# Other places for the hidden weights, a second head with its decay rows in place, and two paced loads

## The chip, the cores and the metric

The kernel runs on one NeuronCore of a Trainium2 chip. The metric is the device time of one execution in microseconds (us). An execution's time is a little longer than the span of its profile, which goes from the first to the last instruction that the profile shows. PE is the matmul engine (TensorE), PEld its weight loads, DVE VectorE, ACT ScalarE, POOL GpSimd, and SP the engine that here issues every DMA.

## The reference

Three layers follow one another, on 4 batches of 576 positions with 512 channels:

```
attention, 8 heads of 64 (32 heads in all):
    cum    = cumsum(max(s, 0))
    scores = q k^T / 8 + min(-(cum_i - cum_j), 0), causal
    x      = softmax(scores) v
gate:      y = (sigmoid(causal conv of x, 5 taps) * (x w_val)) w_out
mixing:    u = y + (y^T U V)^T          over positions, rank 32
MLP:       out = u + relu(u w_ch1) w_ch2        512 -> 2048 -> 512
```

The float64 weights come as pairs of 32-bit words; the kernel widens them itself. For accuracy, most operands are split into a high part (fp32r) and a low part (the rest), and a product takes three matmuls: high by high, high by low, low by high.

## The kernel before

**Attention, heads one after the other.** In step n of one loop the scores of head n and the transposes of head n - 1 are issued, with the products with V after every second head. The decay is folded into the score matmul: each head's Q1 and K1 tiles hold 64 rows of q or k and, from partition 64 on, rows made from cum (K = 68 in all, 4 of them decay rows; 66 for head 0, 2 of them). `score` (L474) makes for each of five row blocks a score matmul into one of six PSUM buffers, a DVE instruction that masks and takes the maximum (a custom DVE operation in the profile, with its result `nm`), and an exponential on ACT; `trans` transposes the result on PE and copies it out. Small fill matmuls go with the transposes up to head 8.

**The decay rows.** For head 0 the row of s is loaded into two partitions (`first`, L239), clipped, scanned, and written into Q1 and K1 in place by two DVE instructions (`row`, L309). For the rest, all 32 rows are clipped, scanned and split on the DVE (L260 to L264), with two multiplications on ACT (L263, L265), in tiles E and F. Heads 1 and 2 get their rows by a DMA straight from E and F (L297, `direct`), the later ones from a copy in DRAM (`ef`).

**The first eight heads** (and two more) take q and k as they are, in `WHOLE`. For the others, `load_raw` (L276) loads q and k into one tile `qk`, ACT rounds it to `hi`, POOL subtracts, and five DMAs (`put`) move the parts into Q1, K1, Q2 and K2. The calls for heads 8 and 9 stand in steps 6 and 7; nothing in the program holds them back before that.

**The order of the work** on each engine isn't the program's. A planner plays the program through with estimated times: each engine takes, of what is ready, what has the highest priority. Priorities follow the program, raised or lowered by kind of work by `PLAN` and, in the first steps, `FIRST`. `later` holds work that the program itself defers. So work without a dependence can move far ahead, and on the chip each engine then keeps the planned order.

**Dense stage and MLP.** For each batch `values`, `outputs` and the mixing run beside the attention of the next, that of the last batch beside the first six MLP blocks. The MLP has 16 hidden blocks m of 128 in groups of 2, 2, 3, 4, 3, 2; within a group it goes through 5 token blocks t (four of 512, one of 256). `ch1` takes u of block t, split into uh and ul by POOL (`split_u`), with w1 of block m; `ch2`, two steps later, multiplies by w2 into accumulators. `widen_w` (L833) makes the four tiles w1h, w1l, w2h, w2l of block m, in ring place m mod 7. Each passes ACT (scale), POOL (limit), DVE (four steps), POOL (round to the high part), POOL (subtract), POOL (low part); it uses two scratch tiles of `scr0` and one of `scr1`, shared by all pieces in program order.

**Memory.** `w0` holds ring places 0 and 1 and is there from the beginning. `wb` (right side) is opened when the values of the last batch are done, and takes the place of their tiles. `ml` (left side) is opened when the dense stage of the last batch is issued, and takes the place of its tiles, in this order: the identity (0.5 KB a partition), w_out high and low (8 KB each), U4 (2.5 KB), V4 high and low (2.3 KB each), the gated values, nh and nl. A tile in `wb` or `ml` waits only for the tiles that stood at its own bytes. Tiles get their place in the order of allocation; `ml` begins with the eight tiles of u for t = 3 (2 KB each).

Of the kernel before, what the change touches and what calls it, by code (L numbers as in the profile page):

```python
# [11 lines left out]
F32 = mybir.dt.float32  # L12
F32R = mybir.dt.float32r
BF16 = mybir.dt.bfloat16
U32 = mybir.dt.uint32
AF = mybir.ActivationFunctionType
ALU = mybir.AluOpType
# [3 lines left out]


PLAN = {
    "pace": ("gpsimd", -500),
    "qk_hi": ("scalar", 6000),
    "qk_lo": ("gpsimd", 2000),
    "put": ("sync", 3000),
# [54 lines left out]
RING = 7  # L82
# [7 lines left out]
ORDER = "T0 T1 S0 T2 T3 S1 S2 S3 T4 S4 A0 A1"  # L90
NPD = 6
DT = {"exp": 0.51, "xh": 0.96, "xl": 0.25, "tap": 1.5, "taps": 0.9, "tanh": 1.83, "gv": 4.3, "nl": 3.6, "rows": 10.0, "prep": 1.51}
WARM = 13


@with_exitstack
def fused_kernel(ctx, tc, qT, kT, vP, s, wval, wout, convw, U, V, w1, w2, rows01, out):
    nc = tc.nc
    B, H, D, S = qT.shape
    P = 128  # L100
# [7 lines left out]
    KP = 4  # L108
# [5 lines left out]
    NH = B * H  # L114
# [99 lines left out]
    w0 = ctx.enter_context(tc.tile_pool(name="w0", bufs=1, side="right", reuse_waits="tile"))  # L214
    at = ctx.enter_context(tc.tile_pool(name="at", bufs=2, side="right"))
# [15 lines left out]
    def part(b, m, n=S, parts=P):  # L231
        return uT[0:parts, m, b * S:b * S + n]

    sp, cum = (part(1, m, parts=NH) for m in range(2))
    ones, first = part(1, 2), part(1, 3)
    E = [part(2, r, parts=NH) for r in range(KP)]
    F = [part(3, r, parts=NH) for r in range(KP)]
    coef = at1.tile([P, 4], F32, name="coef")
    nc.sync.dma_start(first[64:66, :], s[0, 0:1, :].to_broadcast([2, S]))  # L239
    nc.sync.dma_start(coef[64:66, :], rows01)  # L240
    nc.sync.dma_start(sp, s.rearrange("b h s -> (b h) s"))

# [10 lines left out]
    )  # L253
    nc.vector.memset(ones, 1.0)

    nc.vector.tensor_scalar_max(first[64:66, :], first[64:66, :], 0.0)
    nc.vector.tensor_tensor_scan(first[64:66, :], ones[64:66, :], first[64:66, :], 0.0, op0=ALU.mult, op1=ALU.add)
    for t, v in ((E[0], 8.0), (E[2], 8.0), (F[1], 1.0), (F[3], 1.0)):
        nc.gpsimd.memset(t, v)
    nc.vector.tensor_scalar_max(sp, sp, 0.0)  # L260
    nc.vector.tensor_tensor_scan(cum, ones[0:NH, :], sp, 0.0, op0=ALU.mult, op1=ALU.add)
    nc.vector.tensor_copy(F[0].bitcast(F32R), cum)
    nc.scalar.mul(E[1], F[0], -8.0)  # L263
    nc.vector.tensor_sub(F[2].bitcast(F32R), cum, F[0])  # L264
    nc.scalar.mul(E[3], F[2], -8.0)  # L265
    EF = [uT[0:NH, :, b * S:(b + 1) * S] for b in (2, 3)]


# [3 lines left out]
    hd = {}  # L272

    raw = {}

    def load_raw(n):  # L276

        if n < NH and n not in WHOLE:
            b, h = divmod(n, H)
            raw[n] = at.tile([P, S], F32, tag="qk", name="qk")  # L280
            nc.sync.dma_start(raw[n][0:64, :], qT[b, h])
            nc.sync.dma_start(raw[n][64:, :], kT[b, h])

    def load_head(n, direct=False):
        b, h = divmod(n, H)
        t = hd[n] = {"K": 64 + KP if n else 66, "nm": at.tile([P, 6], F32, tag="nm", name="nm")}
        kind = F32 if n in WHOLE else F32R
        for nm in ("Q1", "K1"):
            t[nm] = at.tile([64 + KP, S], kind, tag=nm, name=nm)
        if n in WHOLE:  # L290
            nc.sync.dma_start(t["Q1"][0:64, :], qT[b, h])
            nc.sync.dma_start(t["K1"][0:64, :], kT[b, h])
        else:
            t["qk"] = raw.pop(n)
        if n:
            for i, nm in enumerate(("Q1", "K1")):
                nc.sync.dma_start(t[nm][64:, :].bitcast(F32), EF[i][n:n + 1] if direct else ef[n, i])  # L297

# [5 lines left out]
    def prep_head(n):  # L304

        t = hd[n]
        if n == 0:
            def row(o, i):
                nc.vector.tensor_scalar(  # L309
                    o[64:66, :], first[64:66, :], coef[64:66, 2 * i:2 * i + 1], coef[64:66, 2 * i + 1:2 * i + 2],  # L310
                    op0=ALU.mult, op1=ALU.add,
                )
            return [lambda: row(t["Q1"], 0), lambda: row(t["K1"], 1)]
        if n in WHOLE:
            return []
        t["Q2"], t["K2"] = (at.tile([P, S], F32R, tag=nm, name=nm) for nm in ("Q2", "K2"))
        hi, lo = at.tile([P, S], F32R, tag="hi", name="hi"), t["Q2"]

        def put(o, i):
            Via("put").dma_start(o.bitcast(F32), i.bitcast(F32))  # L320

        def high():
            put(t["Q1"][0:64, :], hi[0:64, :])
            put(t["K1"][0:64, :], hi[64:, :])
            put(t["K2"][0:64, :], hi[64:, :])

        def low():

            put(t["K2"][64:, :], lo[64:, :])
            put(t["Q2"][64:, :], hi[0:64, :])  # L330
        return [
            lambda: rnd("qk_hi", hi, t["qk"]),
            lambda: rest("qk_lo", lo, t["qk"], hi),
            high,
            low,
        ]

    load_head(0)
    load_head(1, True)
    for i in range(2):  # L340
        nc.sync.dma_start(ef[:, i], EF[i])

    for f in prep_head(0):
        f()
    for c in range(5):
        for x in Pt[c]:
            nc.gpsimd.memset(x[:, 0 if c == 0 else CW[c]:], 0.0)
# [33 lines left out]
    def words(ap):  # L381

        return ap.bitcast(U32)
# [40 lines left out]
    pace = []  # L424
# [20 lines left out]
    w12 = {m: {x: w0.tile([P, 512], F32R, tag=f"{x}{m}", name=x) for x in ("w1h", "w1l", "w2h", "w2l")} for m in range(2)}  # L445
# [306 lines left out]
    for n in range(NH + 1):  # L752
        phase[0] = n
        if n > 0:
            pace[:] = [hd[n - 1]["nm"][:, 4:5]]
        if 2 <= n + 1 < NH:
            load_head(n + 1, n == 1)
        load_raw(n + 2)
        if n == 1:
            nc.sync.dma_start(craw.bitcast(U32), words(convw))  # L760
        if 1 <= n <= 3:
            load_wide(n - 1)
        if n < NH and n % 2:
            load_values(n)
        m = n - 1
        items = []

        def add(cost, f, *a):
            items.append((cost, f, a))

        ahead, before = n < NH, n > 0
        for x in (ORDER if m % 2 else ORDER0).split():
            kind, i = x[0], int(x[1])
            if kind == "S" and ahead:
                add((0.1, 0.22, 0.32, 0.42, 0.53)[i], score, n, i)
            elif kind == "T" and before:
                add((0.03, 0.21, 0.32, 0.43, 0.55)[i], trans, m, i)
            elif kind == "A" and before and m % 2:
                add((0.96, 1.7)[i], attn_v, m, i)
        if before and m % 2 == 1:  # L780
            add(0.0, norm, m // 2)
        total = sum(x[0] for x in items)
        if before and m % 2 == 1:
            defer(DT["rows"], lambda pr=m // 2: norm_rows(pr))
        if n + 1 < NH:
            for i, f in enumerate(prep_head(n + 1)):
                defer(DT["prep"] * i, f, "prep")
        todo = 0.0
        if dense:
            first, _, done, _ = dense[0]  # L790
            slots = max(1, first + H - n)
            todo = max(0.0, (DENSE - done) / slots)
        clock["dense"] = clock["att"] = 0.0
        for cost, f, a in items:
            f(*a)
            advance(cost)
            clock["att"] += cost
            if n > 0:
                steps[0] += SIDE[(n > 8) + (n > 12) + (n > 17)] * cost / total
                side_step(int(steps[0]))  # L800
                steps[0] -= int(steps[0])
            run_dense(todo * clock["att"] / total)
        if before and m % H == H - 1:
            dense.append([n + 1, dense_work(m // H), 0.0, clock["now"] + DWAIT])
        force("prep")
        if m % 2:
            hd.pop(m, None)
            hd.pop(m - 1, None)
# [11 lines left out]
    TW = 512  # L820
# [10 lines left out]
            nc.sync.dma_start(raws[k].bitcast(U32), words(w2)[m * P:(m + 1) * P, :] if k % 2 else words(w1)[m])  # L831

    def widen_w(m):  # L833
        pool = w0 if m % RING < 2 else wb if m % RING < 4 else ml
        d = w12[m] = {x: pool.tile([P, TW], F32R, tag=f"{x}{m % RING}", name=x) for x in ("w1h", "w1l", "w2h", "w2l")}

        def part(nm, k):
            scr = [wa.tile([P, TW], F32, tag=f"scr{k}", name=f"scr{k}", bufs=2 - k) for k in range(2)]
            steps = widen(pairs(raws.pop(k)), scr, hi=d[nm + "h"], lo=d[nm + "l"])

            return steps[:6] + [lambda: load_w(k + 2)] + steps[6:]
        return [
            lambda: part("w1", 2 * m), lambda: part("w2", 2 * m + 1),
            lambda: ready.add(m),
        ]
# [97 lines left out]
    wb = ctx.enter_context(tc.tile_pool(name="wb", side="right", **reuse))  # L943
# [6 lines left out]
    ml = ctx.enter_context(tc.tile_pool(name="ml", side="left", **reuse))  # L950
# [50 lines left out]
```

## Time and profile before

| | |
|---|---|
| three timed runs | 766.26, 769.34 (median), 770.9 us |
| the profiled execution | 764.93 us |
| its span | 762.8 us |
| mean granted clock of PE | 0.993 of full speed |
| PE busy | 743.7 us (98%) |
| DVE, ACT, POOL busy | 464.4, 299.2, 291.2 us |

The timed runs and the profiled execution are different executions of the same program. A busy time counts from the start of an instruction to its end; matmuls overlap, so a busy PE is not a PE at its peak. In the views below a line of the timeline has start, duration, engine, line, operation, output <- inputs, shape and count; a bracket at its end is the idle time of the engine just before it and what ended it. L132 is the line of a helper that issues most operations, so they are told apart by their tiles.

### The profile page before, as it was taken

Reading aid. Unit: us, or ns where it says so; the run is one execution under the profiler, and the core shown is the slowest. Engines: PE = TensorE matmul, PEld = TensorE weight load, DVE = VectorE, ACT = ScalarE, POOL = GpSimd, SP = SyncE. Lnnn points to the kernel's source line nnn. Section 1 sums busy time; section 2 is a strip of 40 time slices with the busy share of each in tenths; the row PEclk is TensorE's granted clock in tenths of the full one; section 3 lists DMA queues with packets and bytes.
Section 4 is the critical chain, followed back from the end, with each engine's and each line's share of the span. In section 5 each row is a group of like instructions: output and inputs, shape, how many; then the busy total and the mean of one; then the engine's idle time right before and its main releaser. Section 6 shows DMA issues by size and latency. Waiting matters only on the chain.

```text
span 762.8 us, 12349 instructions
## 1 busy us (share of the span) xinstructions
PE 743.7 (98%) x4453; PEld 624.8 (82%) x4453; DVE 464.4 (61%) x1052; ACT 299.2 (39%) x785; POOL 291.2 (38%) x321
## 2 busy tenths in 40 slices
PE   8999999899999999999899999999999999999998
PEld 4777888788887998798788888888888888888887
DVE  6798875887657755666749996424582234223234
ACT  4777756875677776633212211111121011001110
POOL 3466754553522233557197765102540024100000
PEclk9999999999999999999999999999999999999999
DMA  5734544644455432021103221100120000000023
GB/s 147 229 120 120 140 118 114 174 119 127 120 124 134 122 100 56 18 85 55 56 1 111 83 87 53 54 1 28 55 85 1 0 28 1 1 0 1 1 111 138
DMA packets 27012, 59.40 MB, mean 78 GB/s; under 512 B 4654, under 2 KB 5294, under 8 KB 26952
## 3 DMA queue, kind: packets, MB, share of 16 engines
q1 hardware_dynamic: 26952, 58.62, 26.9%
q8 instruction: 35, 0.57, 0.3%
q14 instruction: 25, 0.20, 0.1%
HBM read 37.04 MB, written 5.31 MB: 56 GB/s over the span
## 4 chain that ended last, share of the span: by engine, by line
PE 85%; DMA 4%; DVE 4%; ACT 3%; issue 2%; SPq 1%; POOL 0%; ACTq 0%; DVEq 0%
PE d L132 39%; PE acc L132 26%; PE pt L132 8%; PE av L132 6%; PE sc L132 6%; DMA qk<-in_kT 2%; DMA K<-Q 1%; DVE av L604 1%; ACT P L132 1%; DVE P L132 1%; DMA Q<-hi 1%; DVE uT L132 1%; DMA uT<-in_w 0%; ACT PTB L132 0%; ACT hi L132 0%
## 5 line engine op out<-in xcount | busy, mean ns | idle before, releaser
L132 PE MATMUL d<-u,w1h 128*128 128x512 f32 (+1 forms) x640 | 184.2, 371 | 0.0
L132 DVE SCALAR_TENSOR_TENSOR hl<-d,hh 128x512 fp32r<-128x512 f32 (+1 forms) x80 | 50.7, 635 | 170.3 <-ACT hh L861 170.3
L861 ACT ACTIVATE hh<-d 128x512 fp32r<-128x512 f32 (+1 forms) x80 | 44.2, 554 | 274.6 <-PE acc L132 149.5
L132 PEld LDWEIGHTS d<-u,w1h 128*128 128x128 f32 x640 | 116.0, 188 | 22.2
L132 PE MATMUL d<-u,w1l 128*128 128x512 f32 (+1 forms) x320 | 118.6, 371 | 0.0
L132 PE MATMUL acc<-hl,w2h 128*128 128x512 f32 (+1 forms) x320 | 105.0, 371 | 0.0
L132 PE MATMUL acc<-hh,w2h 128*128 128x512 f32 (+1 forms) x320 | 104.4, 372 | 0.5 <-DVE uT L132 0.5
L132 PE MATMUL acc<-hh,w2l 128*128 128x512 f32 (+1 forms) x320 | 102.0, 371 | 0.0
L132 ACT ACTIVATE P<-P,nm 64x64 f32<-64x64 f32 (+4 forms) x160 | 89.0, 560 | 25.2 <-DVE nm L132 24.6
L132 PE MATMUL sc<-K,Q 68*128 68x288 f32 (+11 forms) x384 | 89.1, 344 | 4.6 <-ACT PTB L132 1.8
L132 DVE CUSTOM_DVE_ANT_0 P<-sc,causal 64x64 f32<-64x64 f32 (+4 forms) x160 | 65.2, 421 | 30.8 <-PE sc L132 28.2
L132 PE MATMUL pt<-ident,P 128*128 128x128 f32 x480 | 78.5, 284 | 5.4 <-ACT PTA L139 2.6
L132 DVE TENSOR_TENSOR uT<-acc,uT 128x512 f32<-128x512 f32 (+1 forms) x120 | 70.1, 630 | 22.3 <-PE acc L132 22.2
L132 PEld LDWEIGHTS sc<-K,Q 68*128 68x128 f32 (+2 forms) x384 | 62.2, 193 | 13.2 <-ACT PTB L132 2.6
L132 PEld LDWEIGHTS d<-u,w1l 128*128 128x128 f32 x320 | 60.2, 188 | 11.0
L132 PEld LDWEIGHTS acc<-hh,w2h 128*128 128x128 f32 x320 | 58.7, 188 | 12.1 <-issue 0.9
L132 PEld LDWEIGHTS acc<-hl,w2h 128*128 128x128 f32 x320 | 58.8, 188 | 11.2
L132 PEld LDWEIGHTS acc<-hh,w2l 128*128 128x128 f32 x320 | 58.6, 188 | 11.3
L132 PEld LDWEIGHTS pt<-ident,P 128*128 128x128 f32 x480 | 56.3, 145 | 12.3 <-ACT PTA L139 3.6
L604 DVE SCALAR_TENSOR_TENSOR av<-X,cw,av 128x576 f32<-128x576 f32 x64 | 52.3, 817 | 4.9 <-ACT av L132 4.5
L132 DVE SCALAR_TENSOR_TENSOR scr<-raw,scr 128x512 uint32<-128x512 uint32 (+1 forms) x56 | 52.4, 936 | 1.4
L132 DVE TENSOR_SCALAR scr<-scr 128x512 uint32<-128x512 uint32 x56 | 43.3, 773 | 11.9 <-POOL w1l L132 6.3
(123 smaller groups left out, 1286.9 us busy)
## 6 DMA issues: line engine op xcount, KB each, us to landing
raw<-in_w SPq DMA_DIRECT2D x28, 512.0 KB
K<-hi SPq DMA_DIRECT2D x44, 144.0 KB
Q<-hi SPq DMA_DIRECT2D x44, 144.0 KB
V<-in_vP SPq DMA_DIRECT2D x16, 320.0 KB
out<-uT SPq DMA_DIRECT2D x16, 256.0 KB
qk<-in_qT SPq DMA_DIRECT2D x22, 144.0 KB
qk<-in_kT SPq DMA_DIRECT2D x22, 144.0 KB
K<-Q SPq DMA_DIRECT2D x22, 144.0 KB
```

Source lines behind the costliest of these rows:

```text
L132: return f(*args, **kw)
L604: Via("tap").scalar_tensor_tensor(g, X[:, k:k + S], cw[:, p, k:k + 1], g, op0=ALU.mult, op1=ALU.add,)
L861: Via("hh").activation(h_, o, AF.Relu)
```

## The change

- The four tiles of a hidden block stand together no more: in ring places 2 to 6, w2h and w2l are in `wb`, w1h and w1l in `ml`. Before, places 2 and 3 were in `wb` and places 4 to 6 in `ml`, all four tiles of each.
- Head 1 gets its two decay rows in place, as head 0 does, with its own row of s, loaded with head 0's at the start (K = 66). The clipping of these rows and of the 32 rows moves from DVE to ACT. The rows of both heads are issued ahead of the chain for the 32 rows.
- The raw loads of heads 8 and 9 are issued in steps 3 and 4, and each stands behind a POOL copy of one column that reads the last maximum of head 2 or 3.
- 10 instead of 13 warm-up matmuls, and priority 0 for the copies of kind "pace".

```diff
-    "pace": ("gpsimd", -500),
+    "pace": ("gpsimd", 0),
...
-WARM = 13
+WARM = 10
...
-    ones, first = part(1, 2), part(1, 3)
+    ones = part(1, 2)
+    first = [part(0, 0), part(0, 1)]
...
-    nc.sync.dma_start(first[64:66, :], s[0, 0:1, :].to_broadcast([2, S]))
+    for i in range(2):
+        nc.sync.dma_start(first[i][64:66, :], s[0, i:i + 1, :].to_broadcast([2, S]))
...
-    nc.vector.tensor_scalar_max(first[64:66, :], first[64:66, :], 0.0)
-    nc.vector.tensor_tensor_scan(first[64:66, :], ones[64:66, :], first[64:66, :], 0.0, op0=ALU.mult, op1=ALU.add)
-    for t, v in ((E[0], 8.0), (E[2], 8.0), (F[1], 1.0), (F[3], 1.0)):
-        nc.gpsimd.memset(t, v)
-    nc.vector.tensor_scalar_max(sp, sp, 0.0)
-    nc.vector.tensor_tensor_scan(cum, ones[0:NH, :], sp, 0.0, op0=ALU.mult, op1=ALU.add)
-    nc.vector.tensor_copy(F[0].bitcast(F32R), cum)
-    nc.scalar.mul(E[1], F[0], -8.0)
-    nc.vector.tensor_sub(F[2].bitcast(F32R), cum, F[0])
-    nc.scalar.mul(E[3], F[2], -8.0)
+    for x in first:
+        nc.scalar.activation(x[64:66, :], x[64:66, :], AF.Relu)
...
             raw[n] = at.tile([P, S], F32, tag="qk", name="qk")
+            if H <= n < H + 2:
+                Via("pace").tensor_copy(raw[n][:, 0:1], hd[n - H + 2]["nm"][:, 4:5])
...
-        if n:
+        if n > 1:
             for i, nm in enumerate(("Q1", "K1")):
...
-        if n == 0:
+        if n < 2:
+            x = first[n][64:66, :]
...
-            return [lambda: row(t["Q1"], 0), lambda: row(t["K1"], 1)]
+            return [
+                lambda: nc.vector.tensor_tensor_scan(x, ones[64:66, :], x, 0.0, op0=ALU.mult, op1=ALU.add),
+                lambda: row(t["Q1"], 0), lambda: row(t["K1"], 1),
+            ]
...
-    load_head(0)
-    load_head(1, True)
+    for n in range(2):
+        load_head(n)
+    for n in range(2):
+        for f in prep_head(n):
+            f()
+    for t, v in ((E[0], 8.0), (E[2], 8.0), (F[1], 1.0), (F[3], 1.0)):
+        nc.gpsimd.memset(t, v)
+    nc.scalar.activation(sp, sp, AF.Relu)
+    nc.vector.tensor_tensor_scan(cum, ones[0:NH, :], sp, 0.0, op0=ALU.mult, op1=ALU.add)
+    nc.vector.tensor_copy(F[0].bitcast(F32R), cum)
+    nc.scalar.mul(E[1], F[0], -8.0)
+    nc.vector.tensor_sub(F[2].bitcast(F32R), cum, F[0])
+    nc.scalar.mul(E[3], F[2], -8.0)
     for i in range(2):
         nc.sync.dma_start(ef[:, i], EF[i])
-
-    for f in prep_head(0):
-        f()
...
-        load_raw(n + 2)
+        if 3 <= n <= 4:
+            load_raw(n + H - 3)
+        elif n + 2 >= H + 2:
+            load_raw(n + 2)
...
-        if n + 1 < NH:
+        if 2 <= n + 1 < NH:
             for i, f in enumerate(prep_head(n + 1)):
...
-        pool = w0 if m % RING < 2 else wb if m % RING < 4 else ml
-        d = w12[m] = {x: pool.tile([P, TW], F32R, tag=f"{x}{m % RING}", name=x) for x in ("w1h", "w1l", "w2h", "w2l")}
+        d = w12[m] = {
+            x: (w0 if m % RING < 2 else wb if x[1] == "2" else ml).tile([P, TW], F32R, tag=f"{x}{m % RING}", name=x)
+            for x in ("w1h", "w1l", "w2h", "w2l")
+        }
```

## Rows read from the trace of the kernel before

**Rows 1.** The page: busy time by engine, and the chain that ended last.
```profile
PE 743.7 (98%) x4453; PEld 624.8 (82%) x4453; DVE 464.4 (61%) x1052; ACT 299.2 (39%) x785; POOL 291.2 (38%) x321
...
PE 85%; DMA 4%; DVE 4%; ACT 3%; issue 2%; SPq 1%; POOL 0%; ACTq 0%; DVEq 0%
```

**Rows 2.** Stretches: PE, PEld, DVE, ACT, POOL busy (count), PE's granted clock, DMA share, GB/s.
```profile
12.50:16.00 3.50, 3.50 (x16) 2.96 (x17) 0.59 (x4) 1.96 (x9) 0.00 (x0) 0.51 0.98 231
107.00:116.00 9.00, 7.38 (x43) 6.76 (x41) 5.67 (x17) 6.44 (x18) 3.42 (x4) 0.81 0.37 83
...
380.00:402.00 22.00, 22.00 (x114) 18.50 (x113) 10.54 (x21) 2.90 (x6) 19.07 (x23) 1.00 0.04 13
```

**Rows 3.** Timeline of the first 12 us: head 0's rows, scores, maximum, first transpose.
```profile
3.67 1.35 DVE L257 TENSOR_TENSOR_SCAN uT<-uT 2x576 f32<-2x576 f32 x1
...
6.28 0.57 DVE L309 TENSOR_SCALAR K<-uT,coef 2x576 f32<-2x576 f32 x1
...
6.90 3.08 PE L132 MATMUL sc<-K,Q 66*128 66x64 f32 x12 [0.34 <-DVE K L309]
...
8.73 0.68 ACT L263 ACTIVATE uT<-uT 32x576 f32<-32x576 f32 x1 [6.72 <-DVE uT L262]
8.73 0.75 DVE L264 TENSOR_TENSOR uT<-uT 32x576 fp32r<-32x576 f32 x1
...
9.41 0.20 DVE L132 CUSTOM_DVE_ANT_0 P<-sc,causal 64x64 f32<-64x64 f32 x1
...
10.11 0.67 ACT L132 ACTIVATE hi<-qk 128x576 fp32r<-128x576 f32 x1
...
11.16 0.33 PE L132 MATMUL pt<-ident,P 128*128 128x128 f32 x1 [0.96 <-ACT P L132]
```

**Rows 4.** The chain of waits in the first 25 us: start, duration, what held it.
```profile
0.74 1.45 DMA uT<-in_s
...
12.81 4.17 DMA K<-Q
```

**Rows 5.** Timeline: head 1's first score, the next rounding, a transpose behind it.
```profile
12.47 0.60 PE L132 MATMUL sc<-K,Q 68*128 68x64 f32 x2 [0.98 <-DVE nm L132]
...
21.08 0.68 ACT L132 ACTIVATE hi<-qk 128x576 fp32r<-128x576 f32 x1 [1.72 <-DMA qk<-in_kT]
...
22.47 0.66 PE L132 MATMUL pt<-ident,P 128*128 128x128 f32 x4 [0.69 <-ACT P L132]
```

**Rows 6.** Timeline of PE: a gap later in the attention.
```profile
109.79 0.81 PE L132 MATMUL sc<-K,Q 68*128 68x288 f32 x4 [1.61 <-ACT PTB L132]
```

**Rows 7.** PE: last reads of U4 and V4h; matmuls with w1h before 401.2 us.
```profile
377.77 0.39 PE L132 MATMUL d<-nl,U 128*128 128x512 f32 x1
...
381.58 0.29 PE L132 MATMUL d<-V4h,ast 128*128 128x288 f32 x1
...
L132 PE MATMUL d<-u,w1h x80: 277/393/401, 337.9 to 401.0; 128*128 128x512 f32 x64, 128*128 128x256 f32 x16
```

**Rows 8.** Timeline of POOL: weights of hidden blocks 2 to 4, splits of u.
```profile
339.47 0.62 POOL L132 TENSOR_SCALAR w1h<-scr 128x512 fp32r<-128x512 f32 x1
...
362.11 1.71 POOL L132 TENSOR_TENSOR scr<-scr,w2h 128x512 f32<-128x512 f32 x1
...
381.11 2.09 POOL L132 TENSOR_SCALAR u<-uT 128x512 fp32r<-128x512 f32 x4 [13.75 <-DVE uT L703]
383.17 0.62 POOL L132 TENSOR_SCALAR w1h<-scr 128x512 fp32r<-128x512 f32 x1
...
390.15 1.29 POOL L132 TENSOR_TENSOR scr<-scr,w1h 128x512 f32<-128x512 f32 x1
391.40 3.94 POOL L132 TENSOR_TENSOR u<-uT,u 128x512 fp32r<-128x512 f32 x4
```

**Rows 9.** Timeline of the DVE: one step of the widening, twice.
```profile
361.20 0.47 DVE L132 TENSOR_SCALAR scr<-scr 128x512 uint32<-128x512 uint32 x1
...
362.60 1.50 DVE L132 TENSOR_SCALAR scr<-scr 128x512 uint32<-128x512 uint32 x1
```

More of the change, by code (lines that the diff above doesn't have):

```diff
@@ L285, in load_head @@
         b, h = divmod(n, H)
-        t = hd[n] = {"K": 64 + KP if n else 66, "nm": at.tile([P, 6], F32, tag="nm", name="nm")}
+        t = hd[n] = {"K": 64 + KP if n > 1 else 66, "nm": at.tile([P, 6], F32, tag="nm", name="nm")}
         kind = F32 if n in WHOLE else F32R
@@ L306, in prep_head @@
         t = hd[n]
-        if n == 0:
+        if n < 2:
+            x = first[n][64:66, :]
             def row(o, i):
                 nc.vector.tensor_scalar(
-                    o[64:66, :], first[64:66, :], coef[64:66, 2 * i:2 * i + 1], coef[64:66, 2 * i + 1:2 * i + 2],
+                    o[64:66, :], x, coef[64:66, 2 * i:2 * i + 1], coef[64:66, 2 * i + 1:2 * i + 2],
                     op0=ALU.mult, op1=ALU.add,
                 )
-            return [lambda: row(t["Q1"], 0), lambda: row(t["K1"], 1)]
+            return [
+                lambda: nc.vector.tensor_tensor_scan(x, ones[64:66, :], x, 0.0, op0=ALU.mult, op1=ALU.add),
+                lambda: row(t["Q1"], 0), lambda: row(t["K1"], 1),
+            ]
         if n in WHOLE:
```

## The prediction

> **What bounds it.** I read the page first: TensorE's matmul queue (PE) is busy for 98% of the span [rows 1], so any change can only win idle PE time or time at the lower clock. I then cut the span into stretches, to see where the 19 us that are left lie and where the granted clock drops. At 12.5 to 16 us PE is always busy but at a granted clock of 0.51, that is, mostly at 1.2 GHz instead of 2.4; the same drop stands in the stretch from 107 to 116. From 380 to 402 us PE is busy throughout while POOL is busy 19.07 of 22 us [rows 2]. The timeline of the first 11 us shows why the start is slow: the first scores start at 6.90, when the DVE has written head 0's second row, and the first maximum (the custom DVE instruction) starts only at 9.41, when the DVE is through with the chain for all 32 rows [rows 3]. The chain of waits then runs through the loads and moves of head 8, whose turn comes after seven others: 4.17 us of a K<-Q move at 12.81 [rows 4]. So the start is bound by latency, the rest by PE, and the change touches the start and one transition, 380 to 402.
>
> **Head 0.** Before, the DVE clips the row (relu), scans it and writes two rows; now ScalarE clips. The row of s lands at 0.74 + 1.45 = 2.19 [rows 4]. A relu of two rows on ACT is not in the trace; nearest is ACT's pass over 32 rows of the same length, 0.68 [rows 3], so 2.9. Scan 1.35 and two rows of 0.57 each [rows 3] give 5.4 instead of 6.85. One more small load now stands ahead of head 0's Q and K on SP, and when these land is not shown; so the first score starts between 5.4 and 6.9, I take 5.9. ACT had been idle for 6.72 us before its first multiply [rows 3], which covers all three relus; without that cover they would cost 0.68 each. The three warm-up matmuls less end before the first score; they win nothing, since PE waited there.
>
> **Head 1 in place.** The DVE gets a scan and two rows more, 1.35 + 2 x 0.57 = 2.49, and is at 7.9. The chain for all rows (scan, cast, subtraction, from 6.28 + 0.57 = 6.85 to 8.73 + 0.75 = 9.48, so 2.6 us [rows 3]) may stand before the first maximum, which then starts at 10.5, or after it, which then starts at 7.9. Before, it was 9.41. From the first maximum to PE's first transpose it took 11.16 - 9.41 = 1.75, of which 0.67 was ACT rounding head 8's operands ahead of the exponential (hi<-qk at 10.11) [rows 3]. With the loads of heads 8 and 9 paced, that rounding is gone from here: first transpose 1.08 after the maximum, at 9.0 at best, 11.6 at worst, against 11.16. I take the maximum where it was, nearly the middle, hence 10.5: **-0.67** (ends -2.2 and +0.4).
>
> Head 1's first score stood idle 0.98 us behind that transpose, at 12.47 [rows 5], because its rows went by the long chain and a move. In place they are there at 7.9 (10.5 even if both chains went first): **-0.98**, no other end unless the planner puts head 1's rows behind the long chain (0).
>
> **Heads 8 and 9 paced.** Three of their four loads, the rounding and the first moves leave the first 25 us. At 21.08 ACT rounds the next operands after waiting for a load, PE's transpose at 22.47 stands 0.69 idle behind ACT's exponential [rows 5]; nothing late takes its place, as ACT has only exponentials and copies there: **-0.69** (ends -0.69 and 0). The price: two 128x1 copies on POOL that wait for the last maximum of heads 2 and 3, and in SP's queue the Q and K loads of the following heads stand behind the paced ones. Head 8's scores come five heads later; POOL is 38% busy [rows 1]. I take 0; the bad end is one SP stall as long as the one shown, 4.17 [rows 4], of which PE's work on the two heads at hand hides most.
>
> **The clock.** The slow stretch costs 3.5 x (1 - 0.51) = 1.7 us [rows 2]. It followed idles of 0.34, 0.96 and 0.98 us on PE [rows 3, 5]. After the change PE would end head 0's scores at 5.9 + 3.08 = 9.0 [rows 3] and idle until 10.5. That 1.5 is nearest to the gap of 1.61 at 109.79 [rows 6], and there the clock fell too [rows 2]. So I take 0, the good end is -1.7.
>
> **The weights.** The first-layer tiles of ring places 2 and 3 move into the pool that takes the place of the dense stage's tiles; second-layer tiles of places 4 to 6 come out of it. In order of allocation the pool holds eight tiles of 2 KB for block 3, then the two tiles of w1 of hidden block 2. The tiles that stood there were the identity (0.5 KB), the two halves of w_out (16 KB), U4 (2.5 KB) and V4h. So these two tiles lie on U4 and V4h, whose last readers run at 377.77 and 381.58 [rows 7]. Before, POOL wrote w1h of that block at 339.47 [rows 8]; now it can't before 378, and its low part not before 382. The scratch tiles are shared in order, so the rest of places 2 and 3 follows after that. PE needs them late: of the matmuls with w1h, 80 stand before 401.2 [rows 7], which is 10 blocks of 8, all of hidden blocks 0 and 1. The slack is some 19 us for four pieces that take POOL 2 x 0.62 + 2 x 1.29 = 3.8 us each (a limit, taken as long as the rounding, a rounding and two long ones [rows 8]). What is tight is POOL: from 381 to 395 it splits u of the last two blocks (uh and ul), with PE taking each piece as it comes, and three operations on weights between them (two of 0.62, one of 1.29) cost PE nothing [rows 2, 8]. I take **0**, since u went ahead of weights that were ready there; a gain is excluded, since PE has no idle time there to give back [rows 2], and above the end is the third rival.
>
> **Sum.** -0.67 - 0.98 - 0.69 = -2.3 us. The profiled execution took 764.93 (its span 762.8), so 762.6; it lies 4.4 us below the median of the three runs shown, 769.34, and on that median the sum is 767.0. This is the forecast, chance 0.43.
>
> **Rival 1: the start gains all of it.** The planner puts the first maximum ahead of the long chain, the transpose comes at 9.0, PE's idle falls to a few tenths and the clock holds: -2.2 - 0.98 - 0.69 - 1.7 = -5.6, 763.7. For it speaks that the maximum has a high priority in the plan; against it that it had the same before and still came last. Chance 0.2.
>
> **Rival 2: nothing arrives.** The gain at the start is given back because the pieces that set the pace later did not move: head 8's and 9's rounding, two POOL subtractions and ten moves now fall into the stretch where the dense weights are loaded and widened, or the long chain goes first (+0.4) and the clock drop lasts as before. 769.3. Against it: PE holds 85% of the chain of waits [rows 1], so what PE starts earlier mostly ends earlier. The same would come if the change did not do what it says, the paced loads being issued no later than now. Chance 0.17.
>
> **Rival 3: POOL at 382 to 400, slower than before.** If the weights of places 2 and 3 go ahead of the u pieces, POOL has in front of the last split not 2 x 0.62 + 1.29 = 2.5 us but: w1l of block 2 (1.29), the two long operations of w2 (2.6) and of block 3 a limit, a rounding and two long ones (0.62 + 0.62 + 2.6) [rows 8]: 7.7, so it ends 5.2 us later than 395.3. PE can cover one block of the next group, 12 matmuls of 22.0 / 114 us [rows 2], 2.3 us; the buffers let no more run ahead. It idles 2.9 us, and after such a gap [rows 6] the clock costs 9 x (1 - 0.81) = 1.7 more [rows 2]. +4.6 - 2.3: 771.6. It decides from the point where the last u split ends later than 397.6. Chance 0.2. The trace shows what makes it worse: the same DVE step of the widening takes 0.47 us at 361.20 and 1.50 at 362.60 [rows 9], where POOL subtracts from 362.11 to 363.82 [rows 8]. The Trainium skill, GPSIMD Engine Reference, section 1 (Specifications), says that GpSimd's SBUF interfaces are shared with VectorE, with contention against DVE instructions in a two-port mode or with two SBUF inputs. The trace agrees with that, and by that rule the widening would get dearer by being moved from a stretch with an idle POOL into one with a full one; the forecast's 0 holds only as long as the 19 us of slack do.
>
> **Range and chances.** The runs shown spread from 766.26 to 770.9, and the profiled one lies lower still. From rival 1 less 2.7 us for that spread, to rival 3 plus 1.4: 761 to 773. A measurement of this kernel tells 1%, some 7.7 us, from no change. Faster by more than that (below 761.6) needs rival 1 and a lucky base: 0.1. Slower by more (above 777) needs rival 3 with a second stall: 0.05. Within: 0.85.
>
> **What would show it.** Right: first score before 6.2, head 1's first score right behind the first transpose and before 11.2, no qk load before 20 us, no ACT rounding before the exponentials. For the weights: w1h of block 2 written by POOL after 377, PE without idle from 382 to 402. Rival 1: granted clock at full from 10 to 20. Rival 3: u pieces after 398 and idle PE at block 3 or 4. My prediction is wrong if a stall of 3 us or more appears between 25 and 320 us, where I claim that only the order of the same work changes.

## The result, and the profile after

The changed kernel takes 773.58 us (median of 8 runs, 771.95 to 778.55); the kernel before, run beside it, 769.17 (8 runs, 766.26 to 771.66). The ratio is 1.0079, with a 95% interval of 1.0051 to 1.0107: slower, by 3.9 to 8.2 us. The forecast was 767.0, its range ended at 773. The profiled execution took 775.78 us, its span 773.7.

The page, with the lines that answer to [rows 1]:

```profile
PE 748.7 (97%) x4450; PEld 627.5 (81%) x4450; DVE 463.3 (60%) x1053; ACT 300.8 (39%) x788; POOL 292.6 (38%) x323
...
PE 82%; DVE 6%; ACT 5%; DMA 4%; issue 2%; SPq 1%; POOL 0%; ACTq 0%; DVEq 0%; POOLq 0%
```

The engines have nearly the same work: the counts differ by three at most, and DVE, ACT and POOL are busy as long as before to within 1.6 us. PE is busy 5.0 us longer with three matmuls fewer (some of it at the lower clock, below), and the span without PE grew from 19.1 to 25.0 us. In the chain PE holds 82% instead of 85%, ACT and DVE 5 and 6% instead of 3 and 4%. So about half of the 10.9 us between the two spans went to waits. The place of the largest, in the timeline around 44 us (start, duration, engine, line, what; the bracket is the idle time before it and what ended it):

```profile
39.55 0.36 SPq L404 DMA_DIRECT2D uT<-in_wout  x1
39.95 1.74 SPq L278 DMA_DIRECT2D qk<-in_qT  x2
40.27 0.18 POOL L277 COPY qk<-nm 128x1 f32<-128x1 f32 x1
...
41.74 1.23 SPq L279 DMA_DIRECT2D qk<-in_kT  x2
...
46.45 0.68 ACT L132 ACTIVATE hi<-qk 128x576 fp32r<-128x576 f32 x1 [4.57 <-DMA qk<-in_kT]
47.03 0.76 ACT L132 ACTIVATE P<-P,nm 128x576 f32<-128x576 f32 x1
...
47.79 0.74 ACT L132 ACTIVATE PTB<-pt 128x256 f32<-128x256 f32 x2
...
48.21 0.55 PE L132 MATMUL av<-PTB,V 128*64 128x192 f32 x4 [3.85 <-ACT PTB L132]
```

This is the paced load of head 9. The copy that releases it runs at 40.27; of the two issues in each `qk` row one is head 9's and one head 10's, and a load of 512 KB stands ahead of them. Head 9's k is issued at 41.74 and lands at 46.34 (the chain of waits has `41.74 4.60 DMA qk<-in_kT`). In ACT's order the rounding of head 9 (`hi<-qk`) stands directly ahead of the exponential of the head at hand. ACT idles 4.57 us in front of it, though the maximum that the exponential needs had been written by 42.3; the copies PTB come after the exponential, and PE idles 3.85 us in front of the product with V. The Trainium skill, "TensorE: Matmul & The Clock Gate", section on the array's architectural detail, states that ACT's and DVE's queues are strictly first in, first out; these rows agree for ACT.

Stretches of the same trace (PE, PEld, DVE, ACT, POOL busy with counts, PE's granted clock, DMA share, GB/s):

```profile
8.00:14.50 6.50, 6.50 (x22) 4.41 (x21) 4.38 (x17) 4.79 (x16) 0.00 (x0) 0.50 0.50 115
...
48.60:52.00 3.40, 3.40 (x17) 2.27 (x17) 0.00 (x0) 0.64 (x4) 3.15 (x4) 0.51 0.63 156
...
158.00:171.50 13.50, 13.06 (x46) 9.48 (x47) 8.05 (x25) 7.39 (x21) 3.91 (x6) 0.50 0.31 79
...
400.00:422.00 22.00, 22.00 (x109) 18.26 (x108) 14.25 (x21) 4.63 (x9) 17.36 (x18) 1.00 0.15 48
```

Three of them run at 1.2 instead of 2.4 GHz: one at the start (twice as long as before, [rows 2]), one behind the gap at 44, one behind a gap of 1.48 us at 156. The last, which answers to 380 to 402 in [rows 2], is as full as it was.

The start, to be held against [rows 3, 5]:

```profile
2.19 1.25 ACT L259 ACTIVATE uT<-uT 2x576 f32<-2x576 f32 x2 [0.17 <-DMA uT<-in_s]
2.90 2.65 DVE L313 TENSOR_TENSOR_SCAN uT<-uT 2x576 f32<-2x576 f32 x2 [0.83 <-ACT uT L259]
...
6.56 4.86 PE L132 MATMUL sc<-K,Q 66*128 66x64 f32 x12 [1.36 <-DVE K L308]
...
8.79 0.18 DVE L132 CUSTOM_DVE_ANT_0 P<-sc,causal 64x64 f32<-64x64 f32 x1
...
11.64 0.42 PE L132 MATMUL pt<-ident,P 128*128 128x128 f32 x1
11.86 0.53 PE L132 MATMUL sc<-K,Q 66*128 66x64 f32 x2
```

The planner put both heads' scans ahead of both heads' rows, so the first score starts at 6.56 and not at 5.9; and the first twelve score matmuls take 4.86 us instead of 3.08, at the lower clock.

**Where the time went.** Before and after were each profiled again (below). PE multiplies with V after every second head, so pair 1 is heads 0 and 1, and so on. The table cuts each span at PE's first product with V of a pair, at the last batch's first `d<-V4h,ast`, and at the last matmul; after minus before, in us:

| stretch | first profiles | second profiles |
|---|---|---|
| start to pair 1's product (25.33, 24.84 before) | -1.49 | -1.11 |
| to pair 2's (15.05, 15.05) | +0.19 | +1.13 |
| **to pair 3's (16.01, 16.02)** | **+7.53** | **+4.42** |
| to pair 8's (102.13, 103.13) | -2.48 | -2.23 |
| to pair 10's (43.30, 43.69) | +7.71 | +5.39 |
| to the last batch's mixing (177.81, 178.19) | +0.63 | -0.22 |
| MLP (379.85, 379.89) | -1.11 | -1.15 |
| sum | +10.98 | +6.23 |

The runs' ratio gives 6.1 us (0.0079 x 769.17), so the second column is the typical one.

The stretches don't hold the same work, since the planner moved some. First the step from pair 2's product to pair 3's (after, before, and x1, which is the kernel after without the pacing), then from pair 2's product to pair 10's (after, before):

```profile
39.08:62.62 23.54, 19.54 (x131) 14.58 (x130) 14.42 (x47) 14.74 (x45) 10.96 (x13) 0.93 0.56 152
...
40.38:56.39 16.01, 16.01 (x120) 12.23 (x119) 14.48 (x39) 11.55 (x35) 10.29 (x11) 1.00 0.40 126
...
42.29:59.91 17.62, 17.62 (x131) 13.66 (x130) 15.63 (x48) 14.30 (x44) 10.34 (x12) 1.00 0.36 115
...
39.08:213.28 174.20, 160.73 (x1161) 133.83 (x1161) 129.74 (x383) 116.15 (x337) 92.58 (x107) 0.95 0.49 128
...
40.38:201.83 161.45, 155.37 (x1162) 131.87 (x1161) 131.39 (x378) 115.17 (x332) 88.83 (x102) 0.98 0.48 127
```

The step has 11 matmuls more after than before, and in x1 too, where PE does not idle in it: they are worth 1.6 us and are no loss. Against x1 the step lost 5.9 us in the first profile and 2.8 in the second, most of it idle PE (4.0 and 2.5 us) and, in the first, 3.4 us at half the clock. From pair 3's to pair 8's product there are 24 matmuls fewer, from pair 8's to pair 10's 13 more. Taken together, from pair 2's product to pair 10's, the work is the same, and it took 12.8 us longer (7.6 in the second profiles): 7.4 (7.1) of it is idle PE, 5.1 (none) the time at half the clock, halved.

### The profile page after: what moved, and what is told of

The parts are those of the page before. It is cut to its first block, busy times and chain, and to the rows that moved or that the text cites. A ratio compares the mean times of both kernels' runs of the same rounds, so it can differ in the third digit from the quotient of the medians.

```text
span 773.7 us, 12347 instructions
## 1 busy us (share of the span) xinstructions
PE 748.7 (97%) x4450; PEld 627.5 (81%) x4450; DVE 463.3 (60%) x1053; ACT 300.8 (39%) x788; POOL 292.6 (38%) x323
## 4 chain that ended last, share of the span: by engine, by line
PE 82%; DVE 6%; ACT 5%; DMA 4%; issue 2%; SPq 1%; POOL 0%; ACTq 0%; DVEq 0%; POOLq 0%
PE d L132 38%; PE acc L132 26%; PE pt L132 7%; PE av L132 6%; PE sc L132 5%; DMA qk<-in_kT 2%; DVE av L614 2%; DVE uT L132 2%; DMA uT<-in_w 1%; DVE P L132 1%; ACT P L132 1%; ACT PTA L132 1%; ACT uT L132 0%; ACT PTB L132 0%; ACT av L132 0%
## 5 line engine op out<-in xcount | busy, mean ns | idle before, releaser
L132 PE MATMUL sc<-K,Q 68*128 68x288 f32 (+13 forms) x384 | 93.3, 355 | 5.4 <-DVE K L308 1.4
L132 PEld LDWEIGHTS acc<-hl,w2h 128*128 128x128 f32 x320 | 58.9, 188 | 10.9 <-DVE hl L132 0.3
L132 DVE SCALAR_TENSOR_TENSOR scr<-raw,scr 128x512 uint32<-128x512 uint32 (+1 forms) x56 | 54.3, 970 | 1.5
L132 ACT ACTIVATE scr<-raw 128x512 f32<-128x512 f32 x28 | 19.0, 678 | 81.3 <-DMA raw<-in_w 57.7
```

The lines of the kernel that those rows point to most:

```text
L132: return f(*args, **kw)
```

## Experiments

The theories. **A**: ACT, in order, stands at the rounding of head 9 until the paced load has landed, and PE with it. **B**: the weights' new places cost POOL and PE time in the MLP. **C**: any edit makes the planner shuffle the order, and the loss is that. **D**: the paced loads cost it by themselves, through SP's queue. **W**: 10 warm-up matmuls instead of 13 leave the first scores at the low clock. Ratios are to the kernel before on the same chip, with 95% intervals. "Second pair" is the step from pair 2's first product with V to pair 3's, 16.01 us before and 23.54 after.

**x1: the kernel after without the pacing.**

```diff
-            if H <= n < H + 2:
-                Via("pace").tensor_copy(raw[n][:, 0:1], hd[n - H + 2]["nm"][:, 4:5])
...
-        if 3 <= n <= 4:
-            load_raw(n + H - 3)
-        elif n + 2 >= H + 2:
-            load_raw(n + 2)
+        load_raw(n + 2)
```

> The changed kernel with the raw loads of heads 8 and 9 as before (no copies, calls in steps 6 and 7). Theory A (ACT's rounding of head 9 waits 4.57 us for its paced load and holds up the exponentials behind it, PE idles 3.85 us at 44 us and the clock falls): the gap is gone, the second pair of heads takes about 16 us instead of 23.5, and the time is 6 to 8 us below the changed kernel, 766 to 768 where the kernel before has 769. Theory B (the weights' places cost it in the MLP): still 773. Theory C (any change of the program shuffles the plan, and this one was unlucky): still 771 to 775, with its gaps elsewhere.

Measured: 1.0006 (0.9973 to 1.0040). Second pair 17.63 us, no idle PE at 40 to 50, no wait of ACT on the load. That is what A said of the stall. The step stayed above the 16 us expected by the 11 matmuls that the planner had put there, and the ratio is 0.7% below that of the kernel after, some 5.6 us, not quite the 6 to 8.

**x2: the kernel before with the pacing alone** (the lines above added, "pace" at priority 0).

> The kernel before with the paced loads alone. Theory A: slower by 5 to 8 us, 774 to 777 against 769, with an ACT rounding that waits over 3 us for a qk load between 30 and 60 us. Theory B: as before, 769, or 1 to 2 us less from a calmer start. Theory C: anywhere from 766 to 775, with no long ACT wait before 60 us.

Measured: 1.0117 (1.0053 to 1.0180), second pair 21.85. The same place in its timeline:

```profile
41.64 0.19 POOL L283 COPY qk<-nm 128x1 f32<-128x1 f32 x1
...
47.19 0.68 ACT L132 ACTIVATE hi<-qk 128x576 fp32r<-128x576 f32 x1 [2.86 <-DMA qk<-in_kT]
...
48.95 0.91 PE L132 MATMUL av<-PTB,V 128*64 128x192 f32 x4 [2.22 <-ACT PTB L132]
```

The wait came with the pacing, without anything else of the change; 1.6 us of the step are again the 11 matmuls more.

**x3: the kernel before with the weights' places alone.**

```diff
-        pool = w0 if m % RING < 2 else wb if m % RING < 4 else ml
...
+            x: (w0 if m % RING < 2 else wb if x[1] == "2" else ml).tile([P, TW], F32R, tag=f"{x}{m % RING}", name=x)
```

> The kernel before with the weights' places alone. Theory A: no slower; 768 to 769, the attention as before, the MLP 0 to 1 us shorter, as it was in the changed kernel (378.7 us from the mixing of the last batch to the last matmul against 379.9). Theory B: slower by 3 to 6 us, with the loss after 320 us. Theory C: a changed order in the attention too, and gaps there.

Measured: 0.9987 (0.9953 to 1.0021). From the last batch's `d<-V4h,ast` to the last matmul 378.74 us against 379.85: B falls, the places win 1.1 us.

**x4: the kernel before with head 1's rows in place, the relus on ACT and 10 warm-up matmuls** (the kernel after without pacing and weights' places).

> The kernel before with the second head's rows in place, ACT's relus and ten warm-up matmuls, neither paced loads nor moved weights. Theory A: 1 to 2 us faster than before, 767 to 768, since the first product with V came 1.5 us earlier in the changed kernel. Theory B: the same. Theory C: 770 to 775.

Measured: 1.0029 (1.0002 to 1.0057). The gain that A expected did not come: the first product with V is at 26.30 us, 1.0 later than before, with the first scores taking 5.91 us. x1, which lacks the pacing too, has it at 26.36.

**x5: the kernel after, rounding of heads 8 and 9 on POOL.**

```diff
+    "qk_hi2": ("gpsimd", 2000),
...
-            lambda: rnd("qk_hi", hi, t["qk"]),
+            lambda: rnd("qk_hi2" if H <= n < H + 2 else "qk_hi", hi, t["qk"]),
```

> The kernel after, with the rounding of heads 8 and 9 (hi<-qk) on GpSimd instead of ScalarE; the paced loads stay. Theory A (ScalarE, which takes its work in order, stands at this rounding until the paced load has landed, and the exponentials behind it with it): no idle of PE above 1 us between 40 and 50 us (3.85 in the kernel after), the step of the second pair of heads back from 23.5 to some 17.6, ratio to the kernel before 0.998 to 1.003. Theory D (the paced loads themselves cost it, by standing in SP's queue ahead of the loads and moves of heads 4 to 7, whichever engine rounds): the step stays above 21 and the ratio above 1.006. GpSimd may now wait for the load in ScalarE's place; A expects that to cost at most 1 us, since nothing of PE hangs on its next pieces.

Measured: 1.0014 (0.9990 to 1.0039), second pair 19.00. Its timeline shows the same load, as late, and a wait that harms nobody:

```profile
41.24 0.18 POOL L278 COPY qk<-nm 128x1 f32<-128x1 f32 x1
...
44.28 0.78 ACT L133 ACTIVATE P<-P,nm 128x576 f32<-128x576 f32 x1 [0.34 <-DVE nm L133]
...
45.51 0.55 PE L133 MATMUL av<-PTB,V 128*64 128x192 f32 x4
...
47.66 1.14 POOL L133 TENSOR_SCALAR hi<-qk 128x576 fp32r<-128x576 f32 x1 [3.69 <-DMA qk<-in_kT]
```

POOL waits 3.69 us in ACT's place, and the exponential and the product with V start 3.4 and 2.2 us before the load lands. This tells A from D: the load is still paced and late, the stall is gone. PE still idles 0.9 us in the step, so it did not come all the way back to 17.6.

**x7: both paced loads a head earlier** (called in steps 2 and 3, released by the last maximum of heads 1 and 2).

> The kernel after, with both paced loads released one head earlier: by the last maximum of heads 1 and 2 instead of 2 and 3, and called one head earlier. The rounding stays on ScalarE. Theory A says that what costs is not that the load is paced but that it lands after the planner has put the rounding into ScalarE's queue; the planner moves the rounding along with the load, so A expects a wait of ScalarE on the load of 1 to 5 us somewhere between 25 and 45 us and a ratio of 1.003 to 1.012. Theory D expects the stall at the same place as now, since SP's queue is as full. If the ratio is below 1.002, it is the place of the second load behind GpSimd's widening that costs, not the pacing.

Measured: 1.0034 (1.0009 to 1.0059), second pair 17.23. ACT waited 0.79 us for head 8's load at 26.62 and not at all for head 9's, at 36.00; the stall at 44 is gone, and the wait smaller than A expected (1 to 5 us). That its size hangs on what else the queues hold when the load is called is a guess; no run isolates it.

**x8: a third, idle load for heads 8 and 9** (the first 64 rows of q once more, ahead of k).

> The kernel after, with one more load of 64 rows for each of heads 8 and 9 between its two loads (the rows are then overwritten, the output is the same). A larger dose of the suspected cost: the load of head 9 lands some 1 to 3 us later. The planner has the rounding four ScalarE instructions later in this version: behind the last exponential of the head at hand and three copies, ahead of the next copy and exponential. Theory A: ScalarE's wait for the load is still 3 to 6 us, PE idles 2.5 to 5 us at another instruction than now (a transpose or score rather than the product with V), ratio 1.006 to 1.012. Theory D: the stall stays at the same matmul and grows by the load's 1 to 3 us.

Measured: 1.0060 (1.0032 to 1.0087), second pair 20.38. The exponential and three copies that had stood behind the rounding of head 9 are now ahead of it, and so:

```profile
43.80 0.78 ACT L132 ACTIVATE P<-P,nm 128x576 f32<-128x576 f32 x1 [0.53 <-DVE nm L132]
...
45.03 0.55 PE L132 MATMUL av<-PTB,V 128*64 128x192 f32 x4
...
49.06 0.68 ACT L132 ACTIVATE hi<-qk 128x576 fp32r<-128x576 f32 x1 [3.64 <-DMA qk<-in_kT]
...
49.83 1.41 POOL L132 TENSOR_TENSOR Q<-qk,hi 128x576 fp32r<-128x576 f32 x1 [6.52 <-DMA K<-ef]
...
55.20 0.67 ACT L132 ACTIVATE uT<-uT 128x512 f32<-128x512 f32 x1 [1.64 <-POOL wvl L132]
...
56.58 0.66 PE L132 MATMUL pt<-ident,P 128*128 128x128 f32 x4 [1.46 <-ACT P L132]
```

ACT waits 3.64 us, later than in the kernel after, and PE is busy for all of 45 to 50 us. It idles afterwards, from 50 to 61 us: 1.89 us, of that 1.46 at 56.58 in front of a transpose. So A's wait came with its size, A's gap of 2.5 us or more did not: what stands right behind the rounding in ACT's order decides where the wait hits PE. It was not free, though: the step is as long as in the second profile of the kernel after (20.44), and the ratio is in A's range. The rows offer a way round for the rest, which no run tests: POOL, too, stood idle, 6.52 us, in front of the subtraction that reads the rounding's output (the view names a small load, `K<-ef`, as what ended it; the rounding itself ended at 49.74); the weights' pieces behind it came late; ACT waited 1.64 us for one of them (`wvl`) at 55.20, and behind that came the exponential that PE's transpose at 56.58 waited for. D's larger gap at the old place did not come either.

**x9: the rounding held back** by a 128x1 copy on POOL that reads the last maximum of head 6 (7).

> The kernel after, with the rounding of heads 8 and 9 held back: a 128x1 copy on GpSimd into its output, which waits for the last maximum of head 6 (7), stands ahead of it; the paced loads stay as they are. Theory A: the load has long landed when ScalarE comes to the rounding, no wait on it, no idle of PE above 1 us between 40 and 50 us, second pair of heads some 17.6 us, ratio 0.997 to 1.003. Theory D: ratio stays above 1.006. A cost of its own: if the copies by SP that follow the rounding come too late for head 8's scores, PE idles at the first score of head 8 or 9; A expects under 1 us of it.

Measured: 1.0067 (1.0042 to 1.0092), second pair 17.63. The stall at 44 is gone, but the time is not back: held to 62.38, head 8's rounding is too late, and PE waits for the move behind it:

```profile
71.62 0.27 PE L132 MATMUL sc<-K,Q 128*128 128x64 f32 x1 [2.08 <-DMA Q<-hi]
...
79.09 0.77 PE L132 MATMUL pt<-ident,wrs 128*128 128x128 f32 x5 [1.76 <-POOL wrs L132]
```

A's "under 1 us" for that cost was wrong; the stall was moved, not removed.

**x10 to x13: 13 warm-up matmuls** in x5's kernel (x10), in the kernel after (x11) and in x1's (x12); 10 in the kernel before (x13).

```diff
-WARM = 10
+WARM = 13
```

> The kernel after with the rounding of heads 8 and 9 on GpSimd and with 13 warm-up matmuls as before instead of 10. Theory W (with 10 the warm-up ends too early and leaves the first scores at 1.2 GHz: in seven traces with 10 the first twelve score matmuls took 3.4 to 5.9 us, mean 4.9, in three with 13 they took 3.0 to 3.1): first scores 3.0 to 3.2 us, granted clock at full from 7 to 10 us, 1.8 us or more faster than the same kernel with 10 (ratio 1.0014), so a ratio of 0.996 to 1.000; the best of all versions. Rival (the prediction's: PE waits there anyway, the three matmuls win and cost nothing): ratio 1.001 to 1.002 as with 10.

> The kernel after with 13 warm-up matmuls instead of 10, nothing else. Theory A with W: the first scores take 3.0 to 3.2 us instead of 4.86, but ScalarE still stands at the rounding of head 9 for 3 to 5 us between 40 and 48 us and PE idles 2.5 to 4 us: ratio 1.004 to 1.007, that is some 2 us of the 6 come back. Rival: if the warm-up were all of the loss, the ratio would be 1.000.

> The kernel after without the paced loads (rows in place and weights' places stay) and with 13 warm-up matmuls. Theory W: first scores 3.0 to 3.2 us instead of 5.91, ratio 0.996 to 0.999 against 1.0006 with 10. Rival: the planner's new order gives it back, ratio 1.000 to 1.003.

> The kernel before with 10 warm-up matmuls instead of 13, nothing else. Theory W: the first scores take 3.4 to 5.9 us instead of 3.08, the first transpose comes up to 1.5 us later, ratio 1.001 to 1.003. Rival (PE waits there anyway): ratio 0.999 to 1.001 and first scores at 3.1.

Measured, with the first scores' time:

| | warm-up | first scores | second pair | ratio |
|---|---|---|---|---|
| x5 | 10 | 5.92 | 19.00 | 1.0014 (0.9990 to 1.0039) |
| x10 | 13 | 3.08 | 19.22 | 0.9993 (0.9967 to 1.0019) |
| after | 10 | 4.86 | 23.54 | 1.0079 (1.0051 to 1.0107) |
| x11 | 13 | 3.03 | 22.24 | 1.0065 (1.0044 to 1.0086) |
| x1 | 10 | 5.91 | 17.63 | 1.0006 (0.9973 to 1.0040) |
| x12 | 13 | 3.08 | 18.26 | 1.0050 (1.0028 to 1.0072) |
| before | 13 | 3.08 | 16.01 | 1 |
| x13 | 10 | 3.08 | 17.63 | 1.0043 (1.0022 to 1.0063) |

x11 is what A expected: the first scores are quick again, the stall stays (PE idle 2.56 us at 46.65 behind ACT), and most of the loss with it. On the first scores W holds in all traces with 13 (2.98 to 3.08 us) and in all but one with 10 (3.36 to 5.92); the one is x13. That the slow scores are scores at the low clock is read from durations: in x5 all ten warm-up matmuls end 0.43 us apart, in the kernel before the first nine do and the last three 0.21 to 0.22. The granted clock can't show it in x1, x4 and x5: the trace's record of it begins only at 17 us there, and the view gives 1.00 before that. On the time W is not borne out. With 13 the ratio is lower by 0.0014 (x11) and 0.0021 (x10), within the intervals, but x12 came out 0.4% above x1 (their intervals overlap) and x13 0.4% above the kernel before, in plans that differ from their bases' by three matmuls and by the order that the planner then made. x12 has a new gap of 2.52 us at 21.23, in front of a score that waited for `K<-uT`; x13 three gaps of 1.3 to 1.6 us before 26 us. So an edit of three idle matmuls can move this kernel by 0.4% (0.2 to 0.6 in x13), with gaps at places that it doesn't touch: C is real, at that size. The gain by rounding on POOL (0.65 and 0.72%, x5 and x10) is larger than that, the one by leaving the pacing out only with 10 warm-up matmuls (0.73%, x1; 0.15% in x12). x10 beats the kernel after, not the kernel before.

**x14: the two copies on the DVE; the kernel after again.**

```diff
-                Via("pace").tensor_copy(raw[n][:, 0:1], hd[n - H + 2]["nm"][:, 4:5])
+                nc.vector.tensor_copy(raw[n][:, 0:1], hd[n - H + 2]["nm"][:, 4:5])
```

> The kernel after, with the two 128x1 copies that hold the paced loads back on VectorE instead of GpSimd; the order of all TensorE, ScalarE and SP instructions is the same as in the kernel after. There the copy for head 9 waited on GpSimd for a weight's third piece until 40.27 us, while the last maximum of head 3 had ended at 38.4. Theory A: the load is released at 38.5 to 39.6 us (behind the 512 KB load of 39.55 at the latest issue), lands 0.7 to 1.9 us earlier, and PE's idle in front of the product with V shrinks from 3.85 to 2.0 to 3.2 us; ratio lower than the kernel after's by 0.001 to 0.003. Theory C (the loss is the shuffled plan, not this wait): the order is the same, so the ratio is the same within 0.001.

> The kernel after once more, unchanged: the base of x14 on the same chip, and a second profile. Theory A: PE idle for 2.5 to 4 us in front of a product with V at 44 to 48 us again, since it follows from the order of ScalarE's instructions. If the low clock for 13.7 us from 157 on belongs to the plan, it is there again; if to the execution, 3.4 to 7 us of it. Ratio 1.005 to 1.011.

Measured: x14 1.0109 (1.0070 to 1.0148), the kernel after 1.0079 (1.0049 to 1.0110). The dose was not delivered: on the DVE the copy stood behind two later maxima and ran at 40.25, on POOL in this second profile at 40.10. The load landed no earlier, PE's idle was 2.42 and 2.34 us, and the ratios can't be told apart. It speaks neither for A nor for C. The second profile of the kernel after shows the stall again:

```profile
45.76 0.68 ACT L132 ACTIVATE hi<-qk 128x576 fp32r<-128x576 f32 x1 [2.97 <-DMA qk<-in_kT]
...
47.53 0.55 PE L132 MATMUL av<-PTB,V 128*64 128x192 f32 x4 [2.34 <-ACT PTB L132]
```

**The kernel before, profiled twice more.**

> The kernel before once more, unchanged, for a second profile. Its first profile (764.93) lies 4.2 us below the median of its runs. Expected if the stretch at 150 to 171 us is a matter of the execution: 7 to 14 us at the low clock there and an execution of 768 to 771. If of the plan: 3.4 us again.

> The kernel before a third time, unchanged, for the same question: at 150 to 171 us 7 to 14 us at the low clock in an execution of 768 to 771 (execution), or 3.4 us (plan). No idle of PE above 1 us between 25 and 100 us in either.

Measured: executions of 766.21 and 766.46 us; second pair 16.02 and 16.01; at 152 us 6.8 and 3.4 us at the low clock. The kernel after had 13.7 and 6.8. So 6.8 us occurs in both kernels, and the 13.7 of the first profile after, with the 3.4 of the first before, made their difference (10.98 us) larger than that of the runs. How much of this stretch is the plan's stays open.

## Why the prediction was wrong

**The step that failed is "Heads 8 and 9 paced", its price: "I take 0".** The gain was priced by what ACT no longer does in the first 25 us; that came (no `qk` load before 28.54 us, no rounding ahead of the first exponentials). The price was looked for on POOL, which runs the copies, and in SP's queue, as a stall "of which PE's work on the two heads at hand hides most". The rounding was left out: it is moved along with its load, and it waits on ACT, the one engine between PE's scores and PE's products with V. There no work on the heads at hand hides it, since that work stands behind it in the same order. The step with that wait took 2.8 and 5.9 us longer than in x1, which has the same matmuls in it; the 4.4 and 7.5 us of the table hold 1.6 us of moved work besides. Pacing came out slower in all three pairs: 1.0006 to 1.0079 (x1, after), 1 to 1.0117 (before, x2), 1.0050 to 1.0065 (x12, x11; here the intervals overlap). Rounding on POOL took the loss back twice (after to x5, x11 to x10), by 0.65 and 0.72%. [Rows 5] had the sign: at 21.08 ACT stood 1.72 us at a rounding for a load, and a transpose stood behind it. I read that row as a stall that would go, and not as what any rounding close behind its load does. The text's own condition for being wrong, a stall of 3 us or more between 25 and 320 us, is what happened in the first profile (PE 3.85 us, ACT 4.57); in the second ACT waits 2.97 us there and PE 2.34.

**Head 0: half right.** ACT's relu took the 0.68 us taken from [rows 3]. But two scans before the first row cost 1.3 us more than one, so the score came at 6.56, not 5.9. That the warm-up matmuls "win nothing" overlooked that they keep the clock: they ended at 5.19, and the scores took 4.86 us.

**First transpose, -0.67, and head 1, -0.98: smaller.** The first maximum did go ahead of the long chain's end (at 8.79; before, at 9.41), but the first transpose of P stayed late at 11.64 behind the slow scores. Head 1's first score stood right behind it, without its 0.98 of idle, at 11.86 instead of 12.47. Of 2.34 us in all, 1.49 and 1.11 had arrived by the first product with V, in the two profiles. The terms were added as if each came by itself, which the runs don't bear out: the pacing alone (x2) has that product at 25.52 us, the rows without the pacing (x4, x1) at 26.30 and 26.36, where it was at 25.33, 24.84 and 25.18 before.

**The clock, 0.** Wrong at the start: 6.8 us at half speed instead of 3.4, in both profiles of the kernel after, and 3.4 more behind the new gap at 44 in the first. The term was taken from the first 20 us alone; the stretch at 152 to 171 us, 3.4 to 6.8 us at half speed in the profiles before and 6.8 to 13.7 after, is in no term.

**The weights, 0: nearly right.** POOL wrote w1h of block 2 at 394.51, after the readers of its place; PE had no idle at 400 to 422. But I excluded a gain because PE never idles there, and 1.1 us came, in x3 too. The page of x3 has it in the second layer's matmuls (the line of w2l is 102.0 us with a mean of 371 ns in the kernel before):

```profile
L132 PE MATMUL acc<-hh,w2l 128*128 128x512 f32 (+1 forms) x320 | 100.6, 369 | 0.0
```

A busy PE can still have slower and quicker matmuls; why these are quicker stays open.

**The rivals.** Rival 1 failed at the first scores. Rival 2's remark that the moved pieces "now fall into the stretch where the dense weights are loaded and widened" names the right place, but it was priced as a gain given back, not as a loss. Rival 3 had the right sign and the wrong place: its POOL jam at 382 to 400 didn't occur.

**What stays open.** In the table, pairs 8 and 9 took 5.4 to 7.7 us longer and pairs 3 to 7 took 2.2 to 2.5 less. Part of both is a shift over the border between them: 13 matmuls, some 2 us, and the stretch at half the clock, which ends before pair 8's product in the kernel before (at 155.90, the product at 158.53) and behind it in the kernel after (at 171.53, the product at 162.27). What is left is idle PE in other places: of the 7.4 and 7.1 us more between pair 2's and pair 10's products the step with the stall has 4.0 and 2.5. x1, without the pacing, idles 10.5 us there in its one profile, against 6.1 to 7.9 before, so most of this rest isn't the pacing's. The four traces with the attention of the kernel before in its old order (its three, and x3) have 43.3 to 44.1 us for pairs 8 and 9; every trace with another order has 45.0 to 51.0, paced or not. That points to C, but no run isolates the cause. By the runs the pacing is worth most of the 0.79% (x1) or little of it (x12): with orders that move by 0.4% on their own, the stall is shown, its exact share of the loss is not.

## What to carry to other kernels

When a load is delayed, follow its first consumer, not only the load: where another program orders the queues, the consumer may move with the load and wait in front of work on the critical path. Put such a consumer on an engine that nothing critical waits behind (x5), or call the load so early that the wait is short (x7), though neither made this kernel faster than it was before (1.0014 and 1.0034); holding the consumer back by hand moved the stall to its own consumers (x9). And where the order is planned, measure an edit that should do nothing first: here one such moved the time by 0.4%. When stretches of two profiles are compared, count the instructions in them, as the planner may have moved work over the border.

## What the runs showed that I had not expected

Warm-up matmuls that only fill idle time are worth up to 2.8 us of first scores (5.92 against 3.08 us, x5 and x10), as they decide at which clock the scores begin, and yet the whole kernel showed little of it. A copy of one column, put on the DVE to be quicker, ran no earlier than on a busy POOL (40.25 and 40.10), as each engine's order was set with it in another place.
